# Layer one's second mixing product as Strassen block products, with the weights' bounds taken beforehand

## The chip, the cores and the metric

The kernel runs on one core of a Trainium2 chip. The metric is the device time of one execution in microseconds (us), where lower is better. The kernel before takes 1223.19 us, the median of three runs (1223.0 to 1223.26). TensorE (PE in the profile) multiplies matrices, PEld is its loading of weights, VectorE is DVE, ScalarE is ACT, GpSimd is POOL, and SyncE (SP) issues the DMAs. All five take their own instructions in a fixed order and wait for each other by semaphores.

## The reference, cut to what matters

Two layers, each an attention block A and a mixer block B, act on x, which has S = 2048 tokens and D = 1024 features. The change lies in B, whose two products run over tokens.

```python
def _B_ref(x, w1, b1, w2, b2):                        # S, D, F = 2048, 1024, 3584
    h = _layernorm(x, axis=-1)
    u = jnp.einsum("bsd,sf->bdf", h, w1) + b1         # first mixing product
    u = _gelu(u)
    y = jnp.einsum("bdf,fs->bds", u, w2) + b2         # second mixing product
    return (lambda x, *d: x.transpose(*d))(y, 0, 2, 1)

x = x + _A_ref(_layernorm(x, axis=-1), A_wqkv, A_wo)
x = x + _B_ref(_layernorm(x, axis=-1), B_w1, B_b1, B_w2, B_b2)
x = x + _A_ref(_layernorm(x, axis=-1), A_wqkv, A_wo)
x = x + _B_ref(_layernorm(x, axis=-1), B_w1, B_b1, B_w2, B_b2)
```

Both layers use the same weights. Inputs and output are bf16.

## The kernel before

**Order of a layer.** Each of the two layers (`li` 0 and 1, `first` is true for layer one) runs: layer norm, the value projection (`v_proj`, L384), the query and key projections (`qk_chunk`, L399), scores and values of the local attention, the output projection (`out_proj`, L515) with the next norms between its tiles, then B's first product (`gemm1`, L666) and its second one.

**The first product** makes g, the gelu of the hidden units, in 14 feature blocks of 256 (`NFB`, `fb`). Block 0 is plain (L595). Each of blocks 1 to 13 is split two by two (two halves of the features' weights by token parity, two halves of D) and done as seven products of 8 matmuls each by the Strassen-Winograd scheme, 56 instead of 64 (`product`, L719). The operands that are sums of blocks need fp16 and a power of two as scale: in layer one `top` (L685) takes each block's largest magnitude with a VectorE reduction, `share` sends it to all partitions through a small DRAM tile and a broadcasting DMA, `power` (L630 to L638) makes the scale and its inverse of it, ScalarE scales the weights (`scale_w`, L695), and VectorE makes the four sums (`weight_sum`, L609). Partial results go through PSUM banks `s`, `a` and `m`: ScalarE moves a bank's content into the next one (`move`, L728), where the next product adds to it, and `gelu` (L734) ends each quarter. Layer two loads the sums of weights that layer one kept in DRAM.

**The second product of layer one** (`gemm2`, L1013) is plain. It runs over 8 groups i of 256 tokens (`NI`), in each over the two parities c and two halves of D, with 28 matmuls of 128x512 for each quarter: 112 a group, 896 in all (L1021). Each quarter is added to the residual and bias with one VectorE instruction (L1023), and each (c, i) tile of 128 tokens is stored, normed (`stats`: L203, L205 on VectorE, L197 and L198 on ScalarE; `norm_dve` L211) and written transposed into `hT`, which the next layer's value projection reads. Beside it `search` (L1011) takes the largest magnitude of every w2 tile with a VectorE reduction. After the last group `share_w2` spreads these bounds, and `power_w2` makes the scales `cs2` of the groups' weights and `inv2`, their inverses with g's scale in them. `hidden_scale` (L643) makes g's scale `gs` and inverse `gi` at the end of the first product. `zero_q` clears the two tiles `qB` for the attention to come.

**The second product of layer two** (`gemm2s`, L850) does all 8 groups as seven products of 14 matmuls each (L908), 98 a group, two groups interleaved. The token sums of g are T1, T2, T3 and T4; `scale_g` (L744) brings g to fp16's range beforehand and GpSimd makes T3 and T1 (`hidden_sums`) during the first product. The weight sums of a group are A22, S1, S2, S3 and S4, from the raw w2 tiles scaled by `cs2` (L880 on ScalarE, L883 on VectorE). T3 lies in the attention's mask tile `Pm` and in `kT`.

**What sets the order.** `chain_(engine, f, ...)` fixes the order of an engine's steps by hand, and `in_order` does so for TensorE. What isn't chained, a scheduler places. SP issues DMAs one behind the other. Tiles come from pools whose sizes decide when a load can start: `wp` (9 weight tiles), `vhp` (16), `pcp` (2), `x2p` (6), `qp` (2), `gop` (14, g), and two PSUM pairs `s` (4 banks), `a` (2) and `m` (2).

Of the kernel before, what the change touches and what calls it, by code (L numbers as in the profile page):

```python
# [17 lines left out]
P = 128  # L18
# [10 lines left out]
def kernel(  # L29
# [31 lines left out]
    NW2 = 4  # L61
    HF = FT // NW2
# [32 lines left out]
    def two(n):  # L95
        return [bank(n), bank(n)]
# [7 lines left out]
    def st(name, shape):  # L104
        return stat.tile(shape, FP32, name=name, tag=name)
# [51 lines left out]
    mx2 = const.tile([P, NI, NW2], FP32, name="mx2")  # L157
    mx3 = const.tile([P, NI], FP32, name="mx3")
    cs2 = const.tile([P, NI], FP32, name="cs2")
    ncs2 = const.tile([P, NI], FP32, name="ncs2")  # L160
    inv2 = const.tile([P, NI], FP32, name="inv2")
# [20 lines left out]
    mxw = dram.tile([P, NI], FP32, name="mxw")  # L182
# [40 lines left out]
    def chain_(eng, f, *args):  # L223
        with tc.issue_after(last[eng].ins) if eng in last else nullcontext():
            last[eng] = f(*args)
# [417 lines left out]
    def hidden_scale():  # L643
        m = st("gm", [P, 1])
        q = st("gq", [P, 1])
        nc.vector.tensor_reduce(out=m[:], in_=cs[:, 1:], op=ALU.min, axis=AX.X)
        nc.vector.tensor_scalar(out=m[:], in0=m[:], scalar1=2.0 ** -18, scalar2=None, op0=ALU.mult)
        nc.vector.tensor_scalar(out=q[:], in0=cs[:, 0:1], scalar1=0.25, scalar2=None, op0=ALU.mult)
        nc.vector.tensor_tensor(out=gs[:], in0=m[:], in1=q[:], op=ALU.min)
        return nc.vector.reciprocal(out=gi[:], in_=gs[:])  # L650

    def share_w2():
        chain_("DVE", lambda: nc.vector.tensor_reduce(out=mx3[:], in_=mx2[:], op=ALU.max, axis=AX.X))
        t = wp.tile([P, P, NI], FP32, name="bcw", tag="w")
        chain_("SP", lambda: nc.sync.dma_start(out=mxw[:], in_=mx3[:]))
        chain_("SP", lambda: nc.sync.dma_start(out=t[:], in_=mxw[:].partition_broadcast(P)))
        return t

    def power_w2(t):
        powers(0, NI, t[:].rearrange("p q i -> p i q"), cs2, inv2)  # L660
        nc.vector.tensor_scalar(out=inv2[:], in0=inv2[:], scalar1=gi[:], scalar2=None, op0=ALU.mult)
        nc.vector.tensor_scalar(out=ncs2[:], in0=cs2[:], scalar1=-1.0, scalar2=None, op0=ALU.mult)
# [3 lines left out]
    def gemm1(h2, g, first):  # L666
# [34 lines left out]
        def sum_tile(fb):  # L701
            Ss[fb] = qp.tile([P, 4, NI, P], FP16, name="Sw", tag="q")
# [20 lines left out]
        def Tk(n):  # L723
            return [T[:, n, k, :] for k in range(NI)]
# [28 lines left out]

        token_sums()
# [4 lines left out]
        if first:  # L759
            load_w1(2)  # L760
            load_w1(3)
            last[A] = normed[0]
            for c in range(DIL):
                chain_(A, scale_w, 1, c)
            for c in range(DIL):
                chain_(V, top, 3, c)
            share(3)
            sum_tile(1)
            for n in range(4):
                chain_(V, weight_sum, nc.vector, 1, n)  # L770
        else:
            chain_(V, scale_a22, 1)
            load_w1(3)
        load_w1(4)

        for fb in range(1, NFB):
# [13 lines left out]
            if first and more:  # L790
                chain_(A, scale_w, nxt, 0)
            if seek:
                for c in range(DIL):
                    chain_(V, top, far, c)
                share(far)
            chain_(A, move, Z[:], pd)
            in_order(product, pb, Ss[fb][:, 1], Tk(1), False)
            chain_(A, move, pc, pb)
            if fb + 4 < NFB:
                load_w1(fb + 4)  # L800
            in_order(product, pa, a(fb, 1, 0, not first), B21, False)
            chain_(A, gelu, fb, 0, 0, pa, not first)
            if first and more:
                chain_(A, scale_w, nxt, 1)
                sum_tile(nxt)
            in_order(product, pc, Ss[fb][:, 2], Tk(2), False)
            chain_(V, tt, nc.vector, Y[:], Z[:], pc, ALU.add)
            chain_(A, gelu, fb, 1, 1, Y[:])
            if first and more:
                chain_(V, weight_sum, nc.vector, nxt, 0)  # L810
            if first and fb + 2 < NFB:
                chain_(V, power, fb + 3, fb + 4, bc_[fb + 2][:])
            in_order(product, pb, Ss[fb][:, 3], B22, False)
# [7 lines left out]
            hidden_sums(fb - 1)  # L821
            in_order(product, pc, a(fb, 1, 1), Tk(3), False)
            chain_(A, gelu, fb, 1, 0, pc)
        if first:
            chain_(V, hidden_scale)
        hidden_sums(NFB - 1)

    def load_w2(i):
        tiles = []
        for n in range(NW2):  # L830
            t = wt_("w2", [P, HF, 256])
            nc.sync.dma_start(out=t[:], in_=w2_v[:, n * HF:(n + 1) * HF, i * 256:(i + 1) * 256])
            tiles.append(t)
        return tiles
# [175 lines left out]
    def search(i, n, w2t):  # L1010
        return nc.vector.tensor_reduce(out=mx2[:, i, n:n + 1], in_=w2t[n][:], op=ALU.max, axis=AX.XY, apply_absolute_value=True)  # L1011

    def gemm2(c, i, w2t, g, src, dst):  # L1013
        xs = x2("xs")
        nc.sync.dma_start(out=xs[:], in_=rows(src, c, i))
        xo = x2("xo")
        aps = [t[:] for t in two("sasm"[(i * DIL + c) % 4])]
        parts = [(0, 512, aps[0]), (512, 512, aps[1])]
        for lo, w, ap in parts:
            for ft in range(FT):  # L1020
                nc.tensor.matmul(ap, lhsT=w2t[ft // HF][:, ft % HF, c::DIL], rhs=g[ft // GF][:, ft % GF, lo:lo + w],  # L1021
                                 start=(ft == 0), stop=(ft == FT - 1))
            nc.vector.scalar_tensor_tensor(out=xo[:, lo:lo + w], in0=ap, scalar=b2_sb[:, i, c:c + 1],  # L1023
                                           in1=xs[:, lo:lo + w], op0=ALU.add, op1=ALU.add)
        nc.sync.dma_start(out=dst, in_=xo[:])
        mean, rs = stats(xo, 1.0, eps1)
        last["DVE"] = norm_dve(xs[:], xo[:], mean, rs[:])
        nc.sync.dma_start_transpose(out=hT[:, :, cols(c, i)], in_=xs[:])
        for n in range(2 * c, 2 * c + 2):
            chain_("DVE", search, i, n, w2t)  # L1030
# [3 lines left out]
    for li in range(2):  # L1034
# [5 lines left out]
        if first:  # L1040
            start_up(v, wv)
            wts = [None, None]
            chain_("SP", load_qk, 0, wts)
            res = lambda c, i: xin_v[c, i]
        else:
            fill_wv(wv)
            wts = [None, None]
            chain_("SP", load_qk, 0, wts)
            bcw = share_w2()
            for i in range(NI):  # L1050
                for c in range(DIL):
                    v_proj(v, c, i, wv, (0, 1))
            power_w2(bcw)
            res = lambda c, i: rows(xb, c, i)
# [76 lines left out]
        if first:  # L1131
            ln_exp_table()
            hT, qB = new_hT(), new_qB()
            zero_q()
        if not first:
            w1s.clear()
            gemm2s(g, xa[li], out_v)
            continue
        for i in range(NI):
            w2t = load_w2(i)  # L1140
            w1s.clear()
            for c in range(DIL):
                gemm2(c, i, w2t, g, xa[li], rows(xb, c, i))
# [30 lines left out]
```

## Time and profile before

| What | Value |
| --- | --- |
| Median of three runs | 1223.19 us |
| Profiled execution | 1223.0 us |
| Its span | 1221.3 us |
| PE busy | 1205.6 us (99%) |
| DVE busy | 729.6 us (60%) |
| ACT busy | 551.2 us (45%) |
| POOL busy | 108.7 us (9%) |
| First product of layer one starts (L595) | 260.5 us |
| Its block products (L719) | 274.1 to 431.4 us |
| Second product of layer one (L1021) | 431.4 to 624.8 us |
| Value projection of layer two (L384) | 624.8 to 680.0 us |
| Second product of layer two (L908) | 1048.0 to about 1217.5 us |

The span is the time from the first to the last instruction that the profiler recorded. The busy shares are means over stages with different limits, so each stage has to be read by itself. Groups of instructions are printed as line, engine, operation, output and input tiles, shapes and number, then the busy time, the mean duration of one in ns, and the engine's idle time before them with what ended it.

### The profile page before, as it was taken

To read this page: it belongs to the slowest core of one execution; us is meant where nothing else is said; L and a number is where in the kernel's file an instruction comes from. 1 tells how busy PE (TensorE), PEld (TensorE's weight loads), DVE (VectorE), ACT (ScalarE), POOL (GpSimd) and SP (SyncE) were. 2 spreads that over 40 slices of the span, in tenths; PEclk is the share of its full clock that TensorE was granted. 3 is DMA by queue.
4 is the path that set the end of the run, shared out by engine and by line. 5 is a ranking of instruction groups with operands and counts; after the bars stand their busy time and mean duration, and the time that the engine had idled before them with its cause. 6 is when DMAs were issued, how large, how long until landed. Compare 5 with 4: busy or idle time off the path is not lost.

```text
span 1221.3 us, 20012 instructions
## 1 busy us (share of the span) xinstructions
PE 1205.6 (99%) x7946; PEld 559.8 (46%) x8088; DVE 729.6 (60%) x1298; ACT 551.2 (45%) x924; POOL 108.7 (9%) x107
## 2 busy tenths in 40 slices
PE   9999999999999999999999999999999999999998
PEld 4444444444444444444444444444444444444444
DVE  7558887888777346565650467778711212785664
ACT  5457775467666610000013577764543444432342
POOL 0000000290000000000000000002722112200000
PEclk9999999999999999999999999999999999999999
DMA  8922233566565635545520110234946564264520
GB/s 235 153 62 72 82 105 104 165 199 200 167 201 163 203 89 147 135 133 148 162 78 1 44 46 20 77 110 139 309 130 197 155 190 135 72 189 129 154 80 35
DMA packets 217837, 159.28 MB, mean 130 GB/s; under 512 B 46864, under 2 KB 193936, under 8 KB 214416
## 3 DMA queue, kind: packets, MB, share of 16 engines
q1 hardware_dynamic: 217744, 158.01, 44.7%
q8 instruction: 63, 1.03, 0.4%
q14 instruction: 30, 0.25, 0.1%
HBM read 115.49 MB, written 30.43 MB: 119 GB/s over the span
## 4 chain that ended last, share of the span: by engine, by line
PE 98%; issue 1%; DVE 0%; DMA 0%; ACT 0%; DVEq 0%
PE m L399 18%; PE s L719 12%; PE m L515 9%; PE s L1021 8%; PE m L719 8%; PE s L908 7%; PE a L719 6%; PE m L384 5%; PE m L1021 4%; PE a L1021 4%; PE m L908 4%; PE s L288 3%; PE a L908 3%; PE s L595 2%; PE s L430 2%; PE a L288 1%
## 5 line engine op out<-in xcount | busy, mean ns | idle before, releaser
L399 PE MATMUL m<-hT,wqk 128*128 128x512 bf16 x963 | 223.5, 379 | 6.3 <-issue 4.6
L446 DVE TENSOR_TENSOR Pm<-pc,band 32x640 bf16<-32x640 bf16 x256 | 123.6, 483 | 53.9 <-ACT pc L434 47.1
L399 PEld LDWEIGHTS <-wqk 128*128 128x128 bf16 x1024 | 95.3, 98 | 117.9 <-issue 10.7
L1021 PEld LDWEIGHTS <-w 128*128 128x128 bf16 x896 | 87.7, 98 | 105.7
L719 PEld LDWEIGHTS <-Sw 128*128 128x128 f16 x832 | 81.4, 98 | 98.1
L197 ACT ACTIVATE ln<-mv,eps 128x1 f32<-128x1 f32 x64 | 18.9, 295 | 230.4 <-DVE mv L205 185.1
L515 PE MATMUL m<-wo,oT 128*128 128x512 bf16 x500 | 110.8, 379 | 0.9 <-issue 0.3
L1021 PE MATMUL s<-g,w 128*128 128x512 bf16 x439 | 97.5, 379 | 0.5
L719 PEld LDWEIGHTS <-w 128*128 128x128 f16 (+1 forms) x624 | 61.1, 98 | 73.6
L609 POOL TENSOR_TENSOR T<-h 128x512 f16<-128x512 bf16 x16 | 18.4, 1152 | 809.9 <-DMA xr<-xb 560.9
L410 DVE COPY qB<-qs 32x512 bf16<-32x512 bf16 x136 | 38.2, 281 | 72.1 <-ACT qs L406 70.0
L515 PEld LDWEIGHTS <-oT 128*128 128x128 bf16 x512 | 49.6, 98 | 60.6 <-issue 1.9
L719 PE MATMUL s<-T,Sw 128*128 128x512 f16 x288 | 66.1, 379 | 0.0
L434 ACT ACTIVATE pc<-s,shift 128x320 bf16<-128x320 f32 x128 | 60.8, 531 | 11.2 <-PE s L430 11.2
L609 DVE TENSOR_TENSOR py<-pz,m 128x512 f32<-128x512 f32 x14 | 9.6, 688 | 92.5 <-PE m L719 66.2
L1011 DVE TENSOR_REDUCE mx<-w 128x1 f32<-128x1792 bf16 x32 | 63.0, 2010 | 0.0
L406 ACT CAST qs<-m 128x512 bf16<-128x512 f32 x64 | 37.5, 585 | 44.3 <-PE m L399 41.9
L403 ACT CAST kT<-m 128x512 bf16<-128x512 f32 x64 | 37.5, 585 | 41.9 <-PE m L399 38.8
L384 PE MATMUL m<-wv,hT 128*128 128x512 bf16 x251 | 55.2, 379 | 0.3
L522 DVE TENSOR_TENSOR xn<-m,xr 128x512 bf16<-128x512 f32 x64 | 44.1, 689 | 15.2 <-PE m L515 14.6
L719 PE MATMUL m<-T,Sw 128*128 128x512 f16 x224 | 52.9, 379 | 0.0
L719 PE MATMUL a<-h,w 128*128 128x512 bf16 x224 | 52.9, 379 | 0.0
(172 smaller groups left out, 1817.0 us busy)
## 6 DMA issues: line engine op xcount, KB each, us to landing
w<-in_B_w_dram SPq DMA_DIRECT2D x86, 512.0 KB, 5.6
w<-in_B_w_dram SPq DMA_DIRECT2D x32, 448.0 KB, 3.7
sd<-Sw SPq DMA_DIRECT2D x13, 1024.0 KB, 6.3
Sw<-sd SPq DMA_DIRECT2D x13, 1024.0 KB, 4.9
wqk<-in_A_wqkv_dram SPq DMA_DIRECT2D x16, 512.0 KB, 5.0
xa<-xn SPq DMA_DIRECT2D x32, 256.0 KB, 2.2
xs<-xa SPq DMA_DIRECT2D x32, 256.0 KB, 3.0
wo<-in_A_wo_dram SPq DMA_DIRECT2D x8, 512.0 KB, 5.4
```

Source lines behind the costliest of these rows:

```text
L288: r = nc.tensor.matmul(pss_[k][n][:], lhsT=hT[:, kt, cols(*order[k])], rhs=wv[kt // 2][:, kt % 2, n * 512:(n + 1) * 512], start=(kt == 0), ...
L384: nc.tensor.matmul(ps[:], lhsT=hT[:, kt, cols(c, i)], rhs=wv[kt // 2][:, kt % 2, n * 512:(n + 1) * 512], start=(kt == 0), stop=(kt == KD - 1))
L399: mm = nc.tensor.matmul(ps[:], lhsT=wts[part][:, kt, (g % 2) * P:(g % 2 + 1) * P], rhs=hT[:, kt, lo:lo + 512], start=(kt == 0), stop=(kt = ...
L410: nc.vector.tensor_copy(out=qB[u % 2][hp, h, ls], in_=qs[hp, :])
L434: nc.scalar.activation(out=pc[:, 2 * n:2 * n + 2].rearrange("p t h k -> p (t h k)"), in_=ss[n][:, 0:2 * HG * GW], func=ACT.Exp, scale=scal ...
L446: mm = nc.vector.tensor_tensor(out=Pm[rp, :, s0:s0 + HB, r * KG:r * KG + GW].rearrange("p h t k -> p t h k"), in0=pc[rp], in1=mk, op=ALU.mult)
L515: mm = nc.tensor.matmul(ps[:], lhsT=oT[g][:, cols(c, i)], rhs=wo[n][g // 4][:, g % 4, :], start=(g == 0), stop=(g == NG - 1))
L522: return nc.vector.tensor_tensor(out=xn[:, xs_], in0=pss_["o", n][:], in1=xr[:, xs_], op=ALU.add)
L719: r = nc.tensor.matmul(out, lhsT=lhs[:, k, :], rhs=rhs[k], start=start and k == 0, stop=stop and k == NI - 1, skip_group_check=True)
L908: r = nc.tensor.matmul(out, lhsT=lhs[k], rhs=rhs[k][:, cols_], start=start and k == 0, stop=k == K - 1, skip_group_check=True)
L1011: return nc.vector.tensor_reduce(out=mx2[:, i, n:n + 1], in_=w2t[n][:], op=ALU.max, axis=AX.XY, apply_absolute_value=True)
L1021: nc.tensor.matmul(ap, lhsT=w2t[ft // HF][:, ft % HF, c::DIL], rhs=g[ft // GF][:, ft % GF, lo:lo + w], start=(ft == 0), stop=(ft == FT - 1))
```

## The change

`gemm2` with its `load_w2` and `search`, and the sharing of all w2 bounds at the start of layer two, are gone. `gemm2f` takes their place. It does group 0 plainly (`tokens`, 4 quarters of 28 matmuls) and groups 1 to 7 as seven products of 14 matmuls, one group after the other. The norm, store and transposition of each tile stay, now as single chained steps among the others.

The weights' scales are thus needed in layer one before the group's own tiles are there. So w2 is fetched a second time in pieces, first into `Pm` (which is not yet in use for anything else), later into tiles of `vhp` and `pcp`: pieces of 256 KB (128x1024) for groups 1 to 6 and of 128 KB (128x512) for group 7. Each piece gives one column of `mx2`: on ScalarE as the sum of magnitudes (`bound_act`), on VectorE as the largest magnitude (`bound_dve`). ScalarE does two in each of the blocks 1 to 12 of the first product, four in block 13 and the rest in `gemm2f`; VectorE does two, three and three in blocks 11, 12 and 13. `share_w2`, `power_w2` and `finish_w2` now run for two groups at a time, (1,3), (3,5), (5,7), and for (7,8). Group 0's bound, needed in layer two alone, is taken by `search0` during layer two's value projection.

g is now scaled in layer one too: `hidden_scale` moves into block 11, `late_work` scales all g blocks but the last in blocks 11 to 13, and the last follows the first product. T3 is made by GpSimd during group 0, T1, T2 and T4 by VectorE. `zero_q` after the first product becomes `zero_fill` (it clears `Pm` as well) after `gemm2f`.

```diff
+    def share_w2(i0, i1, nb=NB2):
+        n = i1 - i0
+        chain_("DVE", lambda: nc.vector.tensor_reduce(out=mx3[:, i0:i1], in_=mx2[:, i0:i1, 0:nb], op=ALU.max, axis=AX.X))
+        t = pcp.tile([P, P, n], FP32, name="bcw", tag="pc")
+        nc.sync.dma_start(out=mxw[i0][:, 0:n], in_=mx3[:, i0:i1])
+        nc.sync.dma_start(out=t[:], in_=mxw[i0][:, 0:n].partition_broadcast(P))
...
+    def finish_w2(i0, i1):
...
+        chain_("DVE", ts, inv2[:, i0:i1], ci2[:, i0:i1], gi[:])
+        chain_("DVE", ts, ncs2[:, i0:i1], cs2[:, i0:i1], -1.0)
+        chain_("DVE", ts, k[:], cs2[:, i0:i1], gs[:])
+        chain_("DVE", tt, nc.vector, bia[:, i0:i1, 0], b0, k[:], ALU.mult)
+        chain_("DVE", tt, nc.vector, bia[:, i0:i1, 1], b1, b0, ALU.subtract)
+        chain_("DVE", tt, nc.vector, bia[:, i0:i1, 1], bia[:, i0:i1, 1], k[:], ALU.mult)
...
+    def bound_act(i, n, src):
+        return nc.scalar.activation(out=src, in_=src, func=ACT.Abs, accum_out=mx2[:, i, n:n + 1])
...
+    def search0():
+        for n, t in enumerate(load_w2s(0)):
+            nc.vector.tensor_reduce(out=mx2[:, 0, n:n + 1], in_=t[:], op=ALU.max, axis=AX.XY, apply_absolute_value=True)
...
+        def late_work(fb):
+            n = fb - (NFB - 3)
+            for k in ((0, 4), (4, 9), (9, 13))[n:n + 1]:
+                for f in range(*k):
+                    chain_(V, scale_g, f)
+            if n == 1:
+                share_w2(1, 3)
+            if n == 2:
+                power_w2(1, 3)
+                finish_w2(1, 3)
+                share_w2(3, 5)
+            for _ in range((2, 3, 3)[n]):
+                bound(V, again)
...
             chain_(A, move, pb, pa, None if first else cs[:, fb + 1:fb + 2])
             if first and more:
                 chain_(A, scale_w, nxt, 0)
+            elif first:
+                bound(A, again)
...
             chain_(A, move, pc, pb)
+            if first:
+                bound(A, again)
...
             chain_(A, gelu, fb, 1, 1, Y[:])
+            if first:
+                bound(A, again)
...
         if first:
-            chain_(V, hidden_scale)
+            chain_(V, scale_g, NFB - 1)
```

The loop of `gemm2f` over the groups 1 to 7 (shortened; `scaled` is four ScalarE instructions, `mix` two of VectorE, `corner` a ScalarE move and a VectorE addition, `quarter` one VectorE instruction, `ln_stat` a VectorE aggregate and ScalarE's ln and exp, `bounds(n)` up to n magnitude sums on ScalarE as long as pieces are left, j is the next group):

```diff
+            in_order(product, pa, stripes(i, 0, 0), B11)
+            if i > 1:
+                quarter(i - 1, 1, 0, prev)
+                stat_half(i - 1, 1, 0)
+                mvrs[i - 1, 1] = ln_stat(i - 1, 1)
+            chain_(A, move, pb, pa, scale=cs2[:, i:i + 1], bias=bia[:, i, 0:1])
+            if i > 1:
+                ln_norm(i - 1, 1, *mvrs.pop((i - 1, 1)))
+            in_order(product, pd, weights(S1), T1)
...
+                scaled(j, q[j][:, 0], 1, 1)
+            Z = x2("z", [P, 512], FP32)
+            chain_(A, move, Z[:], pd)
...
+                scaled(j, q[j][:, 1], 0, 1)
+            bounds(1)
+            in_order(product, pb, weights(S2), [T2k(k) for k in range(K)], False)
+            mix(S1, A22, S2, ALU.subtract)
+            S3 = S1
+            mix(S4, S4, S2, ALU.subtract)
...
+            chain_(A, move, pc, pb, bias=bia[:, i, 1:2])
...
+                scaled(j, U2[j], 0, 0)
+            bounds(1)
+            in_order(product, pa, stripes(i, 1, 0), B21, False)
+            corner(i, 0, 0, pa, gi[:])
+            stat_half(i, 0, 0)
+            if more:
+                mix(q[j][:, 1], q[j][:, 1], q[j][:, 0], ALU.add)
+            in_order(product, pc, weights(S3), [T3(k) for k in range(K)], False)
+            Y = x2("y", [P, 512], FP32)
+            chain_(V, tt, nc.vector, Y[:], Z[:], pc, ALU.add)
+            quarter(i, 1, 1, Y[:])
+            stat_half(i, 1, 1)
+            if more:
+                mix(U2[j], q[j][:, 1], U2[j], ALU.subtract)
+            in_order(product, pb, weights(S4), B22, False)
+            chain_(V, tt, nc.vector, Z[:], Z[:], pb, ALU.add)
+            quarter(i, 0, 1, Z[:])
+            stat_half(i, 0, 1)
+            bounds(2)
...
+                scaled(j, U4[j], 1, 0)
+            bounds(1)
+            mvrs[i, 0] = ln_stat(i, 0)
+            in_order(product, pc, weights(A22), [T4k(k) for k in range(K)], False)
+            ln_norm(i, 0, *mvrs.pop((i, 0)))
+            prev = pc
+            if i == 1:
+                power_w2(5, 7)
+                finish_w2(5, 7)
...
+            if i == 4:
+                share_w2(7, 8, 2 * NB2)
+            if i == 5:
+                power_w2(7, 8)
+                finish_w2(7, 8)
...
         gemm1(h2, g, first)
         last.pop("SP")
-        if first:
-            ln_exp_table()
-            hT, qB = new_hT(), new_qB()
-            zero_q()
...
+        hT = new_hT()
+        gemm2f(g, xa[li], xb)
+        qB = new_qB()
+        zero_fill()
```

The transformation keeps the values but for rounding: 98 fewer matmuls of 128x512 in all (112 + 7x98 = 798 instead of 896).

## The prediction

> **What bounds the kernel now.** I read the chain of waits first, then the busy table, then the stretches of the stages the change touches, then the groups of their instructions. The chain that ended last says whose time counts:
>
> ```profile
> PE 98%; issue 1%; DVE 0%; DMA 0%; ACT 0%; DVEq 0%
> ```
>
> TensorE is the bound everywhere, so a removed matmul is worth its pitch and any wait of TensorE costs its length. The table of stretches (core span in us; busy us and instruction count of each engine; clock; DMA share) gives the pitch and shows how much room the others have: one block of layer one's first product, the whole second product, the value projection after it, and layer two's second product, which is already done as block products.
>
> ```profile
> 346.20:358.30 12.10, 12.05 (x57) 5.50 (x57) 9.12 (x14) 8.38 (x9) 0.00 (x0) 1.00 0.72 184
> 431.40:624.80 193.40, 192.45 (x880) 87.66 (x897) 114.33 (x126) 9.53 (x33) 0.00 (x0) 1.00 0.49 135
> 624.80:680.05 55.25, 54.99 (x253) 25.05 (x257) 9.27 (x14) 18.43 (x33) 0.00 (x0) 1.00 0.07 20
> 1048.00:1217.50 169.50, 168.92 (x788) 77.47 (x798) 110.49 (x190) 58.40 (x91) 5.79 (x4) 1.00 0.37 108
> ```
>
> The reader should see that the second product's 896 matmuls take 193.40 us, 215.8 ns each, at full clock and without a gap, while ScalarE works only 9.5 us of it. L1011's reductions (63 us of VectorE) are off the chain: removing them frees nothing but room. In a 12.10 us block of the first product ScalarE has 3.72 us free.
>
> The changed stage is made of instruction kinds that layer two's stage shows:
>
> ```profile
> L880 ACT ACTIVATE qa<-w,cs 128x512 f16<-128x512 bf16 x24 | 15.5, 709 | 0.0
> L880 ACT ACTIVATE qa<-w,cs 128x256 f16<-128x256 bf16 x8 | 4.0, 495 | 0.0
> L915 ACT ACTIVATE m<-a,cs 128x512 f32<-128x512 f32 x4 | 2.6, 662 | 0.9 <-PE a L908 0.9
> L914 ACT COPY U<-s 128x512 f32<-128x512 f32 x4 | 2.3, 585 | 8.9 <-PE s L908 8.9
> L918 ACT ACTIVATE tq<-s,b_sb,gi 128x512 f32<-128x512 f32 x4 | 3.1, 778 | 9.7 <-PE s L908 9.7
> L609 DVE TENSOR_TENSOR u<-qa,u 128x1024 f16<-128x1024 f16 x8 | 5.4, 681 | 0.0
> L609 DVE TENSOR_TENSOR U<-U,m 128x512 f32<-128x512 f32 x4 | 2.7, 685 | 2.3 <-PE m L908 2.3
> L609 DVE TENSOR_TENSOR u<-qa,u 128x768 f16<-128x768 f16 x8 | 4.4, 547 | 0.0
> ```
>
> How their durations add up matters most. In the timeline, eight scaled tiles (six of 0.709, two of 0.495 = 5.24 us) took 4.57 us together, and fourteen mixes of 0.406 took 4.76:
>
> ```profile
> 1091.43 4.57 ACT L880 ACTIVATE qa<-w,cs 128x512 f16<-128x512 bf16 x8
> ```
>
> So the next ScalarE instruction starts (5.24-4.57)/7 = 0.097 us before the one before it ends, and the next VectorE one 0.07 to 0.08. A step that needs the one before starts only after its full end.
>
> **The parts.** Against the profiled run's 1223.0 us (span 1221.3 and 1.7 around it; the median shown is 1223.19):
>
> *Matmuls.* Seven groups go from 112 to 7x14 = 98: 98 fewer, x 0.2158 = **-21.15 us**. A group now takes 21.15 us of TensorE.
>
> *Bounds beforehand.* 128x1024 magnitude sums on ScalarE, two a block in first-product blocks 1 to 12, four in block 13; three are VectorE's late on. No row shows a magnitude with an accumulator. Below: 1.14 us, between the rows of 128x512 (0.709) and 128x2048 (1.996, L695); above: 1.24 (L555, 128x1024) plus a small instruction of 0.295 (L197) = 1.54. I take 1.24, the row of its size. ScalarE then works 8.38+2.5 = 10.9 of 12.1 us a block (11.5 at worst): hidden by its free 3.7 us. Their fetches (two issues of about 0.34 us a block on SP, among the weight loads and the broadcasts of column bounds) add 0.5 MB to a block that moves 184 GB/s x 12.1 = 2.2 MB at share 0.72: share 0.88, hidden; six buffers refilled three blocks ahead cover lateness. I cost this 0, at worst 4 (third rival).
>
> *g scaled in layer one.* 14 VectorE instructions of 0.747, the last (g[13]) before matmul 27 of group 0, 26x0.2158 = 5.6 us after the first product. VectorE has queued since 0.6 us before the first product's end: four scales (2.7), eleven small steps for groups 1 and 2 (about 0.2 each, 2.3), a share, three reductions (1.2 each by L1011's slope, 3.5); g[13] is done 8.6-8.7 us in with its own 0.75. TensorE waits 8.65-0.6-5.6 = **+2.4**. Bounds 1.5 (small steps at 0.11) and 4 (a broadcast of the bounds, 1.4 and 3.6 us to landing for its two transfers, still under way when the first small step wants it: everything named here is queued behind that step).
>
> *Ring of a group.* Products hand over banks: move pb (ScalarE) -> its queue to the corner's move -> VectorE's corner, adds, mixes, statistics -> ln and exp -> the next group's move pb, which stands behind ln/exp. With the starts at pitch: ScalarE from pb to the corner's end is pb 0.59, twelve scaled tiles 6.7, Z 0.49, pc 0.59, two bounds of 128x512 1.4, corner 0.78 = 10.55; VectorE to the last aggregate: corner, statistics, two mixes (1.08), Y add, quarter, statistics, two mixes, Z add, quarter, statistics, aggregate 8.1; norm, last quarter, statistics, aggregate 2.9; ln/exp 0.5. Sum 22.05 against 21.15: **+0.7 to 0.9** in groups 2 to 4. Without the two bounds, 20.65 in 5 to 7: nothing. Eleven small steps (2.3) enter VectorE's part of the ring after groups 1 and 5 (+1.3 and +1.0 beyond what slack there was), and T2's 14 mixes of 0.335 stand before the first group's ln/exp (+1.3). Group 7's own tail +1.2 (its memset competes). I take **+7** in all: 3x0.73 + 1.3 + 1.3 + 1.0 + 1.2. Bounds: 2.3 (only the two small-step stretches) and 18 (the ring at full durations, second rival).
>
> *POOL.* T3's fourteen subtractions of 1.15 (16 us) run in group 0. In layer two, a two-input VectorE scaling beside such a subtraction took 1.64 us instead of 0.747. Here T1's 14 mixes begin about when T3 ends; even at 2.2 times their 0.41 they add 6 us with 14 us to go until product pd reads them: 0. The Trainium skill (SBUF — State Buffer, "SBUF: two separate sides") speaks against the change here: a VectorE operation with two SBUF inputs and a GpSimd one exclude each other for the whole instruction. By it every overlapped two-input step would wait up to one subtraction; that is what the 1.64 us show, and the sum would still carry nothing unless T1's room is used up.
>
> *Weights.* Each group's four pieces are issued some 10 us before the first scaled tile reads them; landing took 5.6 us (512 KB): hidden by 4 us.
>
> *Start of layer two.* Group 0's bound for layer two (reductions 3x2.28 + 1.2) and the fill of Pm (2.78) and qB (2x1.78) now stand on VectorE in the middle of group 7's tail. The first value tile needs the m bank that Z's add frees. That add would be ready 3.0 us before the end; ahead of it stand the memset (from 6.5 before), Y add 0.61, reduction 2.2, quarter 0.66, reduction 2.2, statistics 0.61, then itself 0.69: done 3.2 after the end: **+3.3** (0 if the reductions came later, 6 if the second memset too went ahead). The next four value tiles reuse that one bank: each waits for its own cast, 0.2 to see the matmul end, 0.585 (L386), 0.04 = 0.82: 4x0.82 = **+3.3**.
>
> Sum: -21.15+2.4+7+3.3+3.3 = -5.15, so **1218 us**.
>
> **Rivals.**
> 1. *The gain comes nearly whole* (0.17). Idle queues absorb the ring: move pb finds ln/exp done early. For it: layer two's stage with the same kinds runs its 170 us without a gap. Against: there two groups share one pass, and statistics aren't in it. -21.15+2.4+2.3+3.3, and 0 or 3.3 for the shared bank: 1210 or 1213; say 1212.
> 2. *The ring is paid in full durations* (0.25): slower. One mechanism, in move pb's wait for ln/exp: if each step needs the one before, or reads what a DMA brings late, no overlap is gained. ScalarE 12.1 + VectorE 11.0 + ln/exp 0.5 + hand-overs 0.3 = 23.9 in groups with bounds (+2.75 each), 22.5 in the others (+1.3 each): 3x2.75+3x1.3+1.3+2x2.3 = 18 in place of 7: 1229. It decides from 21.15 + (21.15-2.4-6.6)/7 = 22.9 us a group. For it: the stage is one ring through three engines. Against: the timeline's overlaps.
> 3. *The first product pays too* (0.10): a magnitude at 1.54 us stands ahead of a bank's move or a gelu on ScalarE, and TensorE waits 0.3 us in each of 13 blocks: +4, 1222, no change. For it: ScalarE's queue is in order. Against: 0.6 us a block would still be free, and gelus have slack of 0.8 to 1.7 us before them.
>
> Likeliest case 0.48: own range 1214.5 to 1221.5.
>
> **Chances.** A measurement here tells some 0.2% (2.4 us) from no change. Faster: 0.17 + 0.44 of the likeliest + 0.01 = 0.62; within: 0.04 + 0.09 = 0.13; slower 0.25. Range: 1211 (inside rival 1) to 1230 (rival 2 with bounds of 1.0 us, +1).
>
> **What would show it.** 798 matmuls in the stage, still about 216 ns apart at clock 1.00. A gap of about 2.4 us before matmul 27 of group 0, released by the scaling of g on VectorE. Gaps of 0.7 us in groups 2 to 4 whose releaser is ScalarE's move or VectorE's corner, none in 5 but after the small steps. Groups at 21.9 us, not 23.9 (rival 2) or 21.15 (rival 1). The first value tile 3.3 us late behind a VectorE add, then four gaps of 0.8 on ScalarE. ScalarE at about 10.9 of 12.1 us a block; a first product longer than before would make rival 3 right. A first-product stall on a fetch, or a weight piece landing late, would make the prediction wrong altogether.

## The result and the profile after

The changed kernel takes 1274.47 us (median of four runs, 1271.84 to 1275.8), the kernel before 1223.22: a ratio of 1.0414 with a 95% interval of 1.0396 to 1.0433. The forecast was 1218, faster. The profiled execution took 1275.8 us with a span of 1274.0, 52.7 us more than before.

The chain of waits of the changed kernel (first line by engine, second by line or DMA) has lost its single bound:

```profile
PE 70%; DMA 17%; DVE 8%; ACT 4%; issue 2%; SPq 0%; DVEq 0%
PE m L400 17%; PE m L516 8%; DMA mxd<-mx 7%; PE s L767 7%; PE s L980 7%; PE m L385 4%; PE m L767 4%; DMA hT<-kT 4%; PE m L980 4%; PE a L767 3%; PE s L289 3%; PE a L980 3%; PE s L596 2%; PE s L431 2%; DMA bc<-mxd 2%
```

Before, 98% of it was TensorE. Now 17% is DMA, and the second line names two: the 1 KB write of the column bounds in the first product (`mxd<-mx`, with its broadcast `bc<-mxd`) and a transposition in the second (`hT<-kT`). The table of stretches (columns as in the prediction: length, busy us of PE, PEld, DVE, ACT and POOL, granted clock, DMA share, GB/s) says where they fall: blocks 1 to 13 of the first product, group 0, group 3, the stretch around group 6, and the value projection:

```profile
275.10:447.70 172.60, 159.91 (x717) 71.59 (x729) 117.62 (x173) 132.94 (x171) 5.34 (x5) 0.99 0.77 206
447.70:479.70 32.00, 26.80 (x111) 11.56 (x112) 20.60 (x59) 19.99 (x35) 11.75 (x10) 0.89 0.44 119
...
524.70:546.40 21.70, 21.14 (x97) 9.57 (x98) 12.60 (x24) 15.50 (x34) 0.00 (x0) 1.00 0.70 187
...
589.80:641.70 51.90, 21.86 (x89) 9.21 (x88) 12.54 (x32) 11.81 (x23) 0.00 (x0) 0.70 0.53 98
...
669.50:733.00 63.50, 57.28 (x254) 25.45 (x259) 12.37 (x15) 18.95 (x36) 0.00 (x0) 0.97 0.22 22
```

The first row was 157.1 us before; group 3 takes 21.70 us of which TensorE works 21.14, close to the 21.9 of the prediction; in the fourth row TensorE stands for 30 us, which nothing in the prediction has. From the starts of the matmuls, against the kernel before and against 0.2158 us a matmul:

| Stretch | Predicted | Measured |
| --- | --- | --- |
| up to the first product's blocks | 0 | +1.0 |
| 98 matmuls fewer | -21.15 | -21.15 |
| first product, blocks 1 to 13 | 0, at most +4 | +15.3 (172.44 for 157.13) |
| group 0 (g[13] late) | +2.4 | +7.8 (31.96 for 24.17) |
| groups 1 to 7, without the next row | +7 | +8.9 |
| one gap before group 6's third product | not foreseen | +30.1, and 2.8 of half-speed matmuls |
| start of layer two | +6.6 | +7.9 (3.2 and 59.92 for 55.25) |
| sum | -5.15 | +52.7 |

The first row isn't clearly the change's: over the kernels of this case the blocks start anywhere from 274.2 to 275.3 us.

**The 30 us gap.** Three timelines of the changed kernel tell it (start, duration, engine, line, operation, tiles; in brackets what ended the idle time before). SP's queue:

```profile
576.15 0.53 SPq L659 DMA_DIRECT2D mxw<-mx  x1
...
579.26 0.37 SPq L660 DMA_DIRECT2D bcw<-mxw  x1
579.73 42.56 SPq L1170 DMA_TRANSPOSE hT<-kT  x1
622.39 3.82 SPq L918 DMA_DIRECT2D w<-in_B_w_dram  x4
```

VectorE's and ScalarE's:

```profile
593.98 0.21 DVE L1161 BATCH_NORM_AGGREGATE mv<-bn 128x2 f32<-128x12 f32 x1
623.97 0.55 DVE L212 TENSOR_SCALAR kT<-xs,mv,rs 128x1024 bf16<-128x1024 bf16 x1 [29.78 <-DMA hT<-kT]
```

```profile
627.90 0.29 ACT L1163 ACTIVATE ln<-mv,eps 128x1 f32<-128x1 f32 x1 [33.15 <-DVE mv L1161]
628.23 0.20 ACT L1164 ACTIVATE rs<-ln 128x1 f32<-128x1 f32 x1
628.34 0.73 ACT L1135 ACTIVATE s<-s,bia,cs 128x512 f32<-128x512 f32 x1
```

Right after the broadcast of group 7's bound, a transposition that mostly takes 1.24 us sits 42.56 us in SP's queue. The next norm (L212) writes the tile that this transposition still reads, so VectorE waits; behind it stand the statistics, then ln and exp, then the move of the bank (628.34) that TensorE needs. The ring that the prediction traced is what carries the delay to TensorE; the delay came into it by a DMA.

**The first product.** SP's queue over one block, before (first) and after:

```profile
333.95 0.32 SPq L691 DMA_DIRECT2D bc<-mxd  x1
334.94 1.40 SPq L578 DMA_DIRECT2D w<-in_B_w_dram  x1
336.63 0.33 SPq L711 DMA_DIRECT2D sd<-Sw  x1
337.06 0.38 SPq L578 DMA_DIRECT2D w<-in_B_w_dram  x1
341.02 0.32 SPq L689 DMA_DIRECT2D mxd<-mx  x1
346.58 0.32 SPq L691 DMA_DIRECT2D bc<-mxd  x1
```

```profile
345.55 0.34 SPq L739 DMA_DIRECT2D bc<-mxd  x1
345.98 0.39 SPq L689 DMA_DIRECT2D Pm<-in_B_w_dram  x1
346.46 0.46 SPq L579 DMA_DIRECT2D w<-in_B_w_dram  x1
347.01 0.53 SPq L759 DMA_DIRECT2D sd<-Sw  x1
347.63 0.52 SPq L579 DMA_DIRECT2D w<-in_B_w_dram  x1
348.25 4.97 SPq L737 DMA_DIRECT2D mxd<-mx  x1
353.26 0.43 SPq L689 DMA_DIRECT2D Pm<-in_B_w_dram  x1
359.57 0.34 SPq L739 DMA_DIRECT2D bc<-mxd  x1
```

The broadcast must wait until its write has landed, and everything behind it in SP's queue waits too. Before, one turn (broadcast to broadcast) is 12.63 us here and 11.9 on the mean of ten. It goes at TensorE's pace, for in 3.5 us of it the queue stands (337.44 to 341.02) until VectorE has the maxima that the write carries. The list of waits of SP's queue before has this row (us in total, times, longest):

```profile
SPq L689 <- DVE mx L685: 34.5, 10, 3.7
```

After, the write is issued within 3 us of the broadcast, right behind 2.25 MB (a fetch, two weight loads, the store of sums), sits 4.97 us in the queue and has landed 11.3 us after its start. In this turn nothing of the 3.5 us is left (the maxima are ready at 347.63, before the queue comes to the write at 348.25), and it takes 14.0 us.

### The profile page after: what moved, and what is told of

Its sections match the earlier page's. It is cut to its first block, busy times and chain, and to the rows that moved or that the text cites. A ratio compares the mean times of both kernels' runs of the same rounds, so it can differ in the third digit from the quotient of the medians.

```text
span 1274.0 us, 20401 instructions
## 1 busy us (share of the span) xinstructions
PE 1197.0 (94%) x7851; PEld 551.6 (43%) x7990; DVE 754.4 (59%) x1457; ACT 677.4 (53%) x1164; POOL 124.9 (10%) x121
## 4 chain that ended last, share of the span: by engine, by line
PE 70%; DMA 17%; DVE 8%; ACT 4%; issue 2%; SPq 0%; DVEq 0%
PE m L400 17%; PE m L516 8%; DMA mxd<-mx 7%; PE s L767 7%; PE s L980 7%; PE m L385 4%; PE m L767 4%; DMA hT<-kT 4%; PE m L980 4%; PE a L767 3%; PE s L289 3%; PE a L980 3%; PE s L596 2%; PE s L431 2%; DMA bc<-mxd 2%
## 5 line engine op out<-in xcount | busy, mean ns | idle before, releaser
L400 PEld LDWEIGHTS <-wqk 128*128 128x128 bf16 x1024 | 95.1, 98 | 118.0 <-issue 10.7
L435 ACT ACTIVATE pc<-s,shift 128x320 bf16<-128x320 f32 x128 | 60.8, 530 | 11.2 <-PE s L431 11.2
L733 DVE TENSOR_REDUCE mx<-w 128x1 f32<-128x2048 bf16 x22 | 49.8, 2280 | 13.3 <-DMA w<-in_B_w_dram 13.3
L610 POOL TENSOR_TENSOR Pm<-g 128x512 f16<-128x512 bf16 x24 | 27.8, 1175 | 291.6 <-PE a L767 166.9
L556 ACT ACTIVATE h<-xn,bi,rs 128x1024 bf16<-128x1024 bf16 x32 | 39.7, 1241 | 23.1 <-DVE bi L542 23.1
L743 ACT ACTIVATE w<-w,cs 128x2048 f16<-128x2048 bf16 x26 | 51.8, 1996 | 0.0
```

The costliest lines, as they stand in the source:

```text
L400: mm = nc.tensor.matmul(ps[:], lhsT=wts[part][:, kt, (g % 2) * P:(g % 2 + 1) * P], rhs=hT[:, kt, lo:lo + 512], start=(kt == 0), stop=(kt = ...
L435: nc.scalar.activation(out=pc[:, 2 * n:2 * n + 2].rearrange("p t h k -> p (t h k)"), in_=ss[n][:, 0:2 * HG * GW], func=ACT.Exp, scale=scal ...
L556: normed[:] = [nc.scalar.activation(out=h2[c][i][:], in_=xn[:], func=ACT.Identity, bias=t["bi"][:], scale=t["rs"][:])]
L610: return eng.tensor_tensor(out=out, in0=a, in1=b, op=op)
L733: return nc.vector.tensor_reduce(out=bx[fb][:, c:c + 1], in_=w1s[fb][c][:], op=ALU.max, axis=AX.XY, apply_absolute_value=True)
L743: return nc.scalar.activation(out=w[:].bitcast(FP16), in_=w[:], func=ACT.Identity, scale=cs[:, fb + 1:fb + 2])
```

## Experiments

The kernels e1 to e10 were run once each, e11 four times. In the changed kernel, e1, e6 and e7 blocks 1 to 13 are all but alike, and take 172.44, 173.58, 169.63 and 173.38 us: a difference of up to 4 us there says nothing by itself.

**One: the broadcast's shape.** The tile `mxw` is two columns wide, and the shares of one group alone, (7,8) and (0,1), use one of them.

```diff
-    mxw = [dram.tile([P, 2], FP32, name=f"mxw{n}") for n in range(NI)]
+    mxw = {n: dram.tile([P, w], FP32, name=f"mxw{n}") for n, w in ((0, 1), (1, 2), (3, 2), (5, 2), (7, 1))}
```

> The changed kernel with one edit: the DRAM tile through which a single group's bound is shared is 1 wide instead of 2, so that its 128 values lie side by side. Theory (packets): the broadcast of one column out of two is cut into 128x128 pieces of 4 bytes, and the transposition and the weight loads behind it on SP wait for their descriptors; the 30.4 us gap before group 6's third product goes, with some 2.8 us of half-speed matmuls after it: about 1274.5 - 33 = 1241 us, and the packets under 512 B fall by about 2 x 16384 = 32768. Rival (the transposition itself, or reading back a tile just written, is slow): the gap stays, 1272 to 1275 us.

1244.58 us; the gap falls from 30.1 us to 1.0. The lists of DMAs of the changed kernel and of this one (packets; KB each and median us to landing):

```profile
DMA packets 281137, 173.99 MB, mean 137 GB/s; under 512 B 81232, under 2 KB 257360, under 8 KB 277712
...
bcw<-mxw SPq DMA_DIRECT2D x2, 64.0 KB, 43.1
```

```profile
DMA packets 248625, 173.99 MB, mean 140 GB/s; under 512 B 48464, under 2 KB 224848, under 8 KB 245200
...
bcw<-mxw SPq DMA_DIRECT2D x2, 64.0 KB, 4.8
```

32,512 packets fewer at the same bytes, just 2 x (128x128 - 128): each of the two transfers of 64 KB went as 16,384 packets of 4 bytes and landed in 43.1 us, and as 128 rows of 512 bytes in 4.8. So about 29.9 of the 51.3 us that the change cost (31.4 of 52.7 between the profiled spans) hung on the width of a 1 KB tile. All later kernels have this edit.

**Two to four: fetches or magnitude sums?** In e2 the first product's fetches are left out, in e3 ScalarE's sums there, in e4 the fetches go to ScalarE's queue:

```diff
# e2 (skip is set in the first product)
         i, n, nf = jobs.pop(0)
+        if skip:
+            fetched.append((i, n, dst))
+            return
# e3
         i, n, src = fetched.pop(0)
-        chain_(eng, bound_act if eng == "ACT" else bound_dve, i, n, src)
+        if not (eng == "ACT" and refill is not None and refill is not False and refill.__name__ == "again"):
+            chain_(eng, bound_act if eng == "ACT" else bound_dve, i, n, src)
...
+            nc.vector.memset(mx2[:].rearrange("p i n -> p (i n)"), 0.25)
# e4
-        nc.sync.dma_start(out=dst.rearrange("p (f s) -> p f s", s=256),
+        (nc.scalar if len(jobs) >= 20 else nc.sync).dma_start(out=dst.rearrange("p (f s) -> p f s", s=256),
```

> As e1_bounds_contiguous, and the 36 fetches of w2 pieces during the first product are left out (the sums and maxima of magnitudes still run, over whatever the tile holds, so the scales and the output are not the reference's). Theory (the fetches stand ahead of the 1 KB write of the column bounds and delay it): the write lands in 5 to 6 us as before, the first product takes about 171 us instead of 186.3, total about 1241 - 15 = 1226. Rival (ScalarE's two magnitude sums a block delay moves and gelus): the first product stays at 184 to 187 us, about 1241.

> The mirror image: as e1_bounds_contiguous, all fetches stay, and ScalarE's magnitude sums of the first product are left out (a constant stands for their bounds). Theory (fetches): the first product stays at 184 to 187 us, total about 1240. Rival (ScalarE): the first product falls to about 171 us, total about 1226. If both have a part, something between in both runs.

> As e1_bounds_contiguous, with the first product's 36 fetches issued by ScalarE's queue instead of SP's; bytes and sums are unchanged. If standing in SP's queue is what delays the write of the bounds: its landing falls from 10.7 to 5 or 6 us and the first product to 171 to 175 us (two issues of about 0.35 us a block fit into ScalarE's free time), total 1226 to 1231. If it is the bytes on the shared DMA engines: landing stays at 9 to 11 us, first product 182 to 187 us, total 1237 to 1242.

(These expectations count the plain block 0, 13.8 us, with the first product: their 171 and 186 are 157 and 172 in the table.)

| Kernel | Total us | Blocks 1 to 13 | Write's landing, median us |
| --- | --- | --- | --- |
| before | 1223.2 | 157.13 | 5.0 |
| e1 | 1244.58 | 173.58 | 11.2 |
| e2, no fetches | 1229.01 | 157.93 | 7.8 |
| e3, no sums | 1236.25 | 163.35 | 10.0 |
| e4, fetches from ScalarE | 1253.45 | 179.40 | 9.3 |

The sums alone cost 0.8 us, the fetches alone 6.2, both together 12.5 to 16.4: e2's time came out as the theory said, though its write still took 7.8 us to land and not 5 to 6; e3 came out between its two expectations. Where both are there, each seems to stand in the other's loop: in SP's queue a fetch waits until ScalarE's sum has freed its tile (6.3 us of waits in e1), and ScalarE stands for scales that come with the broadcast. e4 was to take the fetches out of SP's way and made it worse; the write still took 9.3 us, and now ScalarE's queue stood too (between its sum's end at 359.8 and the fetch's issue at 362.67 in one block; what that issue waited for isn't shown). So another queue doesn't mend it. Bytes or order was still open.

**Five and nine: the order in SP's queue.** With all bytes and sums kept, SP's steps are written out: the write of the bounds first, the store and the fetches behind it, then the broadcast. e9 moves the weight loads one block ahead:

```diff
# e5
+        def bulk(fb):
+            if first and fb:
+                chain_("SP", keep_sums, fb)
+            for src in due:
+                chain_("SP", fetch, src)
+            due.clear()
...
-        def share(fb):
-            nc.sync.dma_start(out=mxd[fb], in_=bx[fb][:])
+        def share(fb, cur=0):
+            chain_("SP", lambda: nc.sync.dma_start(out=mxd[fb], in_=bx[fb][:]))
+            bulk(cur)
             bc_[fb] = pcp.tile([P, P * DIL], FP32, name="bc", tag="pc")
-            nc.sync.dma_start(out=bc_[fb][:], in_=mxd[fb].rearrange("p c -> (p c)").partition_broadcast(P))
+            chain_("SP", lambda: nc.sync.dma_start(out=bc_[fb][:], in_=mxd[fb].rearrange("p c -> (p c)").partition_broadcast(P)))
...
             if fb + 4 < NFB:
-                load_w1(fb + 4)
+                if first:
+                    chain_("SP", load_w1, fb + 4)
# e9, earlier in the block in place of the last line
+            if first and fb + 4 < NFB:
+                chain_("SP", load_w1, fb + 4)
             if seek:
                 for c in range(DIL):
                     chain_(V, top, far, c)
                 share(far, fb)
```

> As e1_bounds_contiguous (1244.6 us), with SP's order in a block of the first product written out: weight loads, the 1 KB write of column bounds, then the 1 MB store of weight sums and the two fetches of w2 pieces, then the broadcast of the bounds. Bytes and sums are unchanged. Theory (what stands ahead of the write, and a fetch's wait for ScalarE's sum to free its tile, hold SP): the write lands in 5 to 6 us, the first product's blocks 1 to 13 take 157 to 161 us instead of 173.6, total 1229 to 1232. Rival (it is the bytes as such): 170 us or more, total above 1240.

> As e5_bulk_behind_bounds (first product's blocks 1 to 13: 200.2 us), with one more edit of SP's order: a block's two weight loads stand ahead of the write of the bounds of the block before them, one load ahead, as the kernel before has them. Theory: e5's order closed a loop, load -> two maxima -> write -> broadcast -> next load, of 17 us a block; with the load one ahead the loop is open, and since the write lands in 4.6 us the blocks take 157 to 161 us, total 1229 to 1232. Rival (0.5 MB more a block as such): 170 us or more, total above 1240.

e5 took 1271.71 us: the write did land in 4.6 us, yet the blocks took 200.15. VectorE's timeline of e5 says why:

```profile
343.84 4.48 DVE L734 TENSOR_REDUCE mx<-w 128x1 f32<-128x2048 bf16 x2 [7.98 <-DMA w<-in_B_w_dram]
```

The two maxima now wait for a load that stands behind the last broadcast, a loop of 17 us that writing the order out had closed; the scheduler had run the load one ahead. e9 opens it: 1228.85 us, and the blocks take **157.13 us, the time before**, with every fetch and every sum. Its SP queue over a block and the stretch:

```profile
340.97 0.34 SPq L747 DMA_DIRECT2D mxd<-mx  x1
341.36 0.43 SPq L770 DMA_DIRECT2D sd<-Sw  x1
341.88 1.44 SPq L689 DMA_DIRECT2D Pm<-in_B_w_dram  x2
347.00 0.34 SPq L750 DMA_DIRECT2D bc<-mxd  x1
347.76 1.32 SPq L579 DMA_DIRECT2D w<-in_B_w_dram  x2
353.05 0.34 SPq L747 DMA_DIRECT2D mxd<-mx  x1
```

```profile
340.70:352.80 12.10, 12.05 (x57) 5.50 (x57) 9.13 (x14) 10.49 (x14) 0.00 (x0) 1.00 1.07 245
```

At a DMA share of 1.07 (0.72 before in a like block; being above 1, the share must add up packet times that overlap) and ScalarE at 10.49 of 12.10 us, TensorE works without a gap. So the 15 us were neither the bytes as such nor ScalarE's time but the order in SP's queue. Which of the two moves it takes isn't separated: the write ahead of the bulk alone closed another loop (e5), and the loads one ahead alone weren't run. Nor is a quick landing needed by itself: in e9, e10 and e11 the write takes 6.2, 5.7 and 8.6 us to land (medians), and the blocks take 157.13 us in each.

**Six: the start of layer two.** The clearing and the reductions are chained behind group 7's statistics:

```diff
-        zero_fill()
+        chain_("DVE", zero_fill)
...
-            nc.vector.tensor_reduce(out=mx2[:, 0, n:n + 1], in_=t[:], op=ALU.max, axis=AX.XY, apply_absolute_value=True)
+            chain_("DVE", lambda: nc.vector.tensor_reduce(out=mx2[:, 0, n:n + 1], in_=t[:], op=ALU.max, axis=AX.XY, apply_absolute_value=True))
```

> As e1_bounds_contiguous, with VectorE's clearing of the mask and query tiles and the four reductions for group 0's bound chained behind group 7's last statistics. By the prediction's term for the start of layer two (3.2 us of waiting for a bank behind them, then five casts at some 0.85 each): the value projection goes from 60.2 + 3.2 us to 55.5 to 57, total 1237 to 1239. Rival (the last tiles' transpositions or the banks as such set it): at least 62 us with the first gap, total above 1243.

1230.95 us; the value projection takes 55.25 us, as before the change, without a gap. (4 us of the total are the first product, whose loop ran from 169.6 to 173.6 us in kernels that are alike there.) VectorE in the changed kernel shows what was moved:

```profile
663.25 2.78 DVE L176 MEMSET Pm<- 128x3264 uint32 x1 [1.07 <-PE m L1130]
665.95 0.63 DVE L610 TENSOR_TENSOR y<-z,m 128x512 f32<-128x512 f32 x1
666.49 2.27 DVE L710 TENSOR_REDUCE mx<-w 128x1 f32<-128x2048 bf16 x1
668.68 0.74 DVE L1150 SCALAR_TENSOR_TENSOR xs<-y,inv,xs 128x512 bf16<-128x512 f32 x1
669.34 2.28 DVE L710 TENSOR_REDUCE mx<-w 128x1 f32<-128x2048 bf16 x1
671.53 0.68 DVE L1156 BATCH_NORM_STATS2 bn<-xs 128x6 f32<-128x512 bf16 x1
672.13 0.67 DVE L610 TENSOR_TENSOR z<-z,m 128x512 f32<-128x512 f32 x1
```

This is the prediction's list in its order; TensorE goes on at 672.86, 3.2 us late (predicted 3.3).

**Seven and eight: the queues in the second product.** g[13] is scaled before the small steps and reductions, and ScalarE's bank move stands ahead of the last group's ln and exp; e8 is e5, e6 and e7 together.

```diff
             if n == 2:
-                power_w2(1, 3)
-                finish_w2(1, 3)
-                share_w2(3, 5)
...
             chain_(V, scale_g, NFB - 1)
+            power_w2(1, 3)
+            finish_w2(1, 3)
+            share_w2(3, 5)
+            for _ in range(3):
+                bound(V, again)
...
+            chain_(A, move, pb, pa, scale=cs2[:, i:i + 1], bias=bia[:, i, 0:1])
             if i > 1:
                 quarter(i - 1, 1, 0, prev)
                 stat_half(i - 1, 1, 0)
                 mvrs[i - 1, 1] = ln_stat(i - 1, 1)
-            chain_(A, move, pb, pa, scale=cs2[:, i:i + 1], bias=bia[:, i, 0:1])
```

> As e1_bounds_contiguous, with two changes of order: g[13] is scaled before the small steps and reductions for groups 1 to 4, and ScalarE's move into the third product's bank stands ahead of the ln and exp of the group before (of group 0's last tile too). By the prediction's terms: the 4.5 and 0.85 us gaps in group 0 go with 2.6 us of half-speed matmuls behind them, and of the groups' gaps of 0.8 to 2.2 us (13 us in all, less 0.2 each) most: 10 to 14 us less, total 1231 to 1235. Rival (the ring is closed by ScalarE's and VectorE's work, not by ln and exp): the gaps of 0.77 to 0.84 stay, 7 to 9 us less, total 1236 to 1238.

> e5, e6 and e7 together on e1_bounds_contiguous; nothing is left out. If the three act in different places they add up: 1244.6 - 13 - 6.5 - 11 = 1214 us, 1208 to 1220. If one stage's gain returns as a wait in the next (the first product finishes earlier and the w2 pieces are later than it): above 1222.

e7 took 1240.11 us, e8 1258.08. Group 0 falls from 31.4 us to 24.2 in e7, and groups 2 to 6 from 23.4, 21.7, 21.7, 21.15, 22.3 to 20.9, 21.15, 21.15, 21.15, 21.4: the gaps between groups are gone, so ln and exp closed the ring, and the rival of e7's expectation falls. But group 1 grew from 25.3 to 32.8, with gaps of 2.65 and 4.74 us. By ScalarE's timeline the move behind the first gap (480.38) still stands behind ln and exp of group 0's first tile, which had waited 7.2 us for VectorE, and four scaled tiles. The move behind the second (492.66) stands behind ln and exp of group 0's last tile, which waited 3.7 us for VectorE, and eight scaled tiles, one of which waited 1.6 us for its weights. Behind the two gaps, some 18 matmuls start at half speed (about 4 us). Hence 4.5 us less in all, not 10 to 14. e8 keeps e5's loop (201.9 us) and so misses its sum; its second product takes 182.98 us.

**Ten and eleven: all together.** e10 is e9, e6 and e7 with group 2's loads earlier and group 1's moves ahead of the scaled tiles; e11 moves three more steps of group 1, as its expectation says.

> e9, e6 and e7 together, and for group 1: group 2's weight tiles are fetched right after group 0's last product, and ScalarE's moves for group 1's banks stand ahead of the scaled tiles of group 2. Nothing is left out. Theory: first product 157 to 161 us, group 0 24.8, groups 1 to 7 148 to 153, value projection 55.3: total 1223.2 - 21.15 + 1 to 9 = 1203 to 1211 us. Rival (some of it comes back, as in e8 where group 1 had a gap of 6.9 us): 1212 to 1222.

> e10_all_mended (1209.9 us; its second product takes 180.3 us, with gaps of 2.5 and 4.1 us around group 1 and some 2 us of half-speed matmuls) with three steps moved: the small steps for groups 3 and 4 go from group 0 to the end of group 1, so that VectorE makes T1 and T2 4 us earlier; ScalarE moves group 1's bank before group 0's ln and exp and S4's scaled tiles; the corner of group 1 stands ahead of eight of group 2's scaled tiles. Theory (only these queues are late there): second product 172.2 + 1 to 3 us, total 1203 to 1206 us. Rival (VectorE's work in group 1 is too much, about 20 us beside 21.15): a gap of 2 us or more stays somewhere in groups 1 and 2, 1206 to 1210.

e10 took 1209.88 us: first product 157.13, second 180.26 and value projection 55.25. e11 takes **1208.74 us** (four runs, 1208.55 to 1208.88) beside 1223.06 for the kernel before: a ratio of 0.9884, 95% interval 0.9867 to 0.9900, 14.3 us faster than before. Its stretches (first product's blocks, second product, value projection):

```profile
275.10:432.20 157.10, 157.10 (x730) 71.20 (x729) 116.70 (x173) 134.27 (x172) 5.11 (x5) 1.00 1.04 226
432.20:610.00 177.80, 172.71 (x799) 78.06 (x798) 122.04 (x258) 109.29 (x219) 12.30 (x10) 1.00 0.69 181
610.00:665.30 55.30, 55.30 (x258) 25.09 (x257) 18.40 (x24) 18.77 (x34) 0.00 (x0) 1.00 0.10 23
```

5.6 us of the second product are still waits, gaps of 2.0, 3.4 and 0.8 us in groups 1 and 2. So e11's rival held (1206 to 1210). Its reason fits too: the first of these gaps waits for VectorE, which is busy in 19.80 of the 19.94 us from 456.36 to 476.30; the second waits for a bank move behind an ln that stood 4.57 us for VectorE's statistics, and these came behind the small steps for groups 3 to 6. No run takes VectorE's work away there, so that this stays a reading of the trace.

## Why the prediction was wrong

- *Matmuls*: right. 798 at 215.8 ns; a group without waits takes 21.15 us, as group 5 does.
- *The ring*: right in mechanism and nearly in size (7 foreseen, 8.9 measured). Groups 3 and 4 lost 0.55 us each (0.73 forecast), group 5 nothing, group 2 2.2 (0.73 + 1.3), all near the forecast. Group 1 lost 4.2 for 1.3: one of group 2's weight pieces also came 2.3 us late for ScalarE (491.88), which the prediction had hidden by 4 us and had named as a sign of being wrong altogether. The second rival (full durations, 23.9 us a group) is refuted by 21.70, the first (nearly the whole gain) by the gaps.
- *g[13]*: right in mechanism, mis-sized: 5.1 us of waiting for 2.4, because the small steps waited for their broadcast until 452.25. That is the case named as the upper bound, and it went over its 4 us: the broadcast was issued 8.2 us after its write, for a landing taken at 1.4. The sum was short by itself, too: the parts it lists (2.7, 2.3, 3.5 and 0.75) add up to 9.25 us and not to 8.65. Behind the wait came 2.6 us of half-speed matmuls, which I had no term for.
- *POOL*: right, nothing. T1's fourteen mixes ran from 470.05 to 474.82, after T3's last subtraction (464.9), so that this kernel has no overlap in which the two could hold each other up.
- *Start of layer two*: right, 7.9 for 6.6; the casts cost 1.05 less 0.22 each, as forecast.
- *Bounds beforehand*: the first step that failed: "share 0.88, hidden". ScalarE's price was right (1.24 taken; the row of the sums shows 1.052 and 0.193 for reading the accumulator). But I held bytes against a mean share, where the thing to read was one turn of SP's queue: broadcast, loads, write, landing, broadcast again. With the fetches and the sums in it, the write's median time to landing went from 5.0 to 10.7 us, the 3.5 us in which the queue had waited for VectorE were no longer enough, and a turn took 14.1 us on the mean in a stage whose block is 12.1. e9 shows that the share itself sets no limit there: it is 1.07, more than the 0.88 forecast, and there is no wait.
- *The shares*: the second step that failed, and the larger: I priced their transfers once, at 1.4 and 3.6 us from a contiguous row of 8 groups, and took the single-group shares for hidden without looking at the access pattern. The diff has it: `mxw[i0][:, 0:n]` of a tile 2 wide with n = 1. The Trainium skill has the rule that applies (DMA: Bandwidth & Descriptors, "Rules for kernel authors"): a last dimension that isn't contiguous becomes one descriptor per element. The runs agree: 16,256 packets more for each such transfer, and 43.1 us in place of 4.8.
- *Third rival* (the first product pays): right place, wrong cause and size: not ScalarE's time (e9 keeps every sum), and 15 us for 4.

The terms that went wrong sum up: 30.1 + 2.8 + 15.3 + 5.4 (group 0) + 1.9 (ring) + 1.3 (start) + 1.0 (ahead of it) = 57.8, and the forecast span was 1216.2.

## What to carry to other kernels

Before adding transfers to a queue that has a wait in each turn, follow one turn, from a wait to the same wait in the next, and see in how much of it the queue stands for another engine (3.5 of some 12 us here). The length of the turn alone doesn't tell, since a queue that has room goes at the stage's pitch all the same; nor does the mean DMA share. In e9 a small write that others wait for ahead of the bulk, together with loads one turn ahead of what waits, mended the stage; the first without the second made e5 slower. Look at the access pattern of each new small transfer as closely as at that of a large one.

## What else the runs showed of the hardware

- TensorE's clock falls after long waits. After group 0's gap of 5.3 us the granted clock is 0.50 over the next 5.6 us, then 1.00 (two stretches of the changed kernel):

```profile
458.40:464.00 5.60, 5.34 (x13) 1.93 (x14) 0.00 (x0) 5.60 (x12) 5.60 (x6) 0.50 0.28 62
464.00:470.00 6.00, 6.00 (x29) 2.70 (x28) 2.91 (x13) 2.69 (x6) 0.94 (x1) 1.00 0.08 25
```

Matmuls then start every 0.43 us. Over all runs every gap above 3.5 us (from one matmul's start to the next) was followed by 5 to 13 such matmuls and none below 2.6 us; between them both are seen (2.63 us with, 3.35 us in e11 without). At 0.21 us more for each, a gap above 3.5 us so costs some 1 to 2.7 us more than its length. The Trainium skill (TensorE: Matmul & The Clock Gate, "What's actually happening") says that activity is judged over a window of 3.4 us which runs freely.

The traces' clock records agree, and show more. In each run the stretches at 0.50 begin whole multiples of 3.413 us apart, wherever the gaps fall: in the changed kernel the first begins at 412.77 us and the next ones 13, 56 and 76 such steps later. Laid over the 87 gaps in which TensorE stands for 1.5 us or more (from 250 us on), this grid sorts them. Where TensorE stood for 64% or more of a step the next step ran at 0.50, and where it was 62% or less it stayed at 1.00; two steps lie at 63%, one of each kind. So 2.42 us of standing, 71% of one step, halved the clock in the changed kernel (from 409.92), while 3.25 us in e4 (from 501.06), 46% of one step and 49% of the next, didn't. A step at 0.50 in which a gap still took 24% or more was followed by a second one, at 21% or less by full speed.
- One DMA in 4-byte packets held back more than itself: the transposition issued behind it took 42.56 us to issue (1.24 us mostly), and four weight loads stood behind that.
